# Reordering the middle of a fused attention-and-MLP training step: exponential, wo transposes, d(o) by head, and dV groups between the sums

## The chip, the cores and the metric

The kernel runs on one core of a Trainium2 chip. A core has TensorE (PE), VectorE (DVE), ScalarE (ACT), GpSimd (POOL) and SyncE (SP), each with its own instruction queue, and 16 DMA engines between its on-chip memory (SBUF, and PSUM for PE's results) and HBM. The metric is the device time of one execution in microseconds, less is better; of several runs, the median. The profile and the trace come from one further, profiled execution.

## The reference

One decode token goes through a block with adaptive layer norm. `_f` is the forward pass; the kernel returns its output and the gradients of nine inputs.

```python
mod = (_silu(c) @ w_mod).reshape(1, 6, 1, -1)            # sa, ca, ga, sb, cb, gb
h = _layernorm(x) * (1 + ca) + sa
q = (h @ wq) as 32 heads of 192
o = softmax(q k^T * 192**-0.5) v                          # k, v: 32 x 8192 x 192
x = x + ga * (o @ wo)                                     # x: 1 x 640
h = _layernorm(x) * (1 + cb) + sb
x = x + gb * (h + _gelu(_layernorm(h) @ w3) @ w4)         # w3: 640 x 1536, the shifted branch is zero for one token
_out, _vjp = jax.vjp(_f, A_x, A_k_cache, A_v_cache, A_wq, A_wo, B_w3, B_w4, c, w_mod)
```

All tensors are bfloat16. K and V are 100.7 MB each, and so are their gradients.

## The kernel before

The work has three parts. The **first part** walks over the 32 heads: K and V come in halves of 1.5 MB, DVE and PE form the scores, ACT the exponentials (`E_all`), and PE sums V times the exponentials (`mp`, from the scaled V tiles `vs`). The **last part** walks back from head 31 in 64 steps of half a head. A step `s` multiplies V by d(o) on DVE (`mul_q`, L1028, two quarters), sums the products on PE with an identity matrix (`tree_q`, L1047, 12 matmuls a quarter into `dot_ps`, a pool of one buffer), makes dP (L344) and dS (L1345) on DVE, dK from dS on DVE (`dk_part`, L1063), and dV as eight groups of outer products on PE (`dv_groups`, L1058) that ACT copies out (L1059). dK and dV are stored from POOL, V is loaded from SP; the buffer for step `s + 4` comes free when the second product of step `s + 1` has been read.

The **middle**, from about 530 to 590 us, has to be done once and in sequence: the last heads' softmax, the output projection (`pair_ao`), the second layer norm (`n2_bf`), `w3` (`u_ps`, L817), GELU, `w4` (`h2_ps`, L900), and back: d(g) by twelve DVE pieces (`dg_part`, L504; pieces not yet done are taken in order, so a call with `NF` does all that are left), `du_bf`, d(n2) (`dn_ps`, L904), the backward layer norm in closed form (`pr`, its means, `s4`, `q4`, `qr`) to `dao_bf` (L942), and d(o) for the first pair of heads (`do_mm(TL)`, L1004, from the transposed `wo` of `do_t`, L886). Work that is not in this sequence is put between: `mp` units for head 30 (`m_units`: two `main`, L402, and two `rest`, L407), transposes of w3 (`w3t`, nine calls, L800 and ACT copies L801, two PSUM buffers), scaled V rows on ACT (`vs_act`, L644), the sums of M2 (`m_add`), the blocks of dW4 (`dw4_dve`, L872, twelve of 128 x 640) with their stores, and the small outputs (`dx1_out`, `d_sb_out`).

The order on PE, DVE, ACT and SP is the order of the program text: a manual schedule holds for `ORDER = {PE, DVE, Activation, SP}`. POOL's queue is ordered by the planner. An instruction waits at the head of its engine's queue and holds all behind it. `psB`, which holds `do_ps`, and `psS`, which holds `c_ps` and the means, have one buffer for their tag; `dv_ps` has two.

Between the middle and the loop over steps, the first step's beginning is written out: `mul_q(0, 0)`, four dV groups and their store, `tree_q` of the first quarter, `mul_q(0, 1)`, the products `cx` and their sums `cs` (L1324, L1326), the matmul `c_ps` (L1328), three dW4 blocks, `cpr` (L1331, a scalar for each head that dS needs), `tree_q` of the second quarter, and `mul_q(1, 0)`. In step 0 the loop does the other four groups, and 1 to 7 by the list `gs = [1, 3, None, None, 5, None, 7, None]`.

Of the kernel before, what the change touches and what calls it, by code (L numbers as in the profile page):

```python
# [20 lines left out]
def kernel(  # L21
# [26 lines left out]
    nc = tc.nc  # L48
# [308 lines left out]
    with tc.tile_pool(name="vs", bufs=3) as vsp, tc.tile_pool(name="ft", bufs=2) as ft, \  # L357
# [38 lines left out]
        def m_units(q, kb, vs, mp):  # L396
            j0 = (q % 2) * JQ
            z = q == 3

            def main(lo, hi):  # L400
                for k in range(lo, hi):
                    T_.matmul(mp[:, 0:MW], lhsT=kb[:, j0 + k, 0:P], rhs=vs[:, k, 0:MW], start=(q == 0 and k == 0), stop=(z and k == JQ - 1), skip_group_check=True)  # L402

            def rest(lo, hi):
                for k in range(lo, hi):
                    p0 = 64 * (k % 2)
                    T_.matmul(mp[p0 : p0 + 64, MO : MO + MW], lhsT=kb[:, j0 + k, P:DH], rhs=vs[:, k, 0:MW], start=False, stop=(z and k >= JQ - 2), skip_group_check=True)  # L407
# [101 lines left out]
        with tc.manual_schedule(engines=ORDER):  # L509
# [209 lines left out]
            T_.matmul(po[:, 4:6], lhsT=c32, rhs=os2[:, 2 * DH : 2 * DH + 2], start=True, stop=True)  # L719
            for k in range(3):  # L720
                T_.matmul(po[:, k : k + 1], lhsT=os2[:, k : 2 * DH : 3], rhs=c32[:, 0:1], start=True, stop=True)
            pe.pop(0)()
# [5 lines left out]
            V_.tensor_tensor(out=xP, in0=xP, in1=xc0, op=ALU.add)  # L728
            V_.reciprocal(out=rinv[:, 2 * TL : 2 * TL + 2], in_=po[:, 4:6])
# [50 lines left out]
            dg_part(1)  # L780
# [4 lines left out]
            vs_act(vs3, 3, 8, 12)  # L785
# [43 lines left out]
            V_.tensor_tensor(out=e1, in0=e1, in1=u, op=ALU.mult)  # L829
            dg_part(1)  # L830
            pe.pop(0)()
            pe.pop(0)()
            w3t()
            pe = m_units(3, ky[1], vs3, mp)
            pe.pop(0)()
            w3t()
            pe.pop(0)()
            w3t()
            V_.tensor_scalar(out=w_, in0=w_, scalar1=1.0, scalar2=None, op0=ALU.add)
            V_.reciprocal(out=s_, in_=w_)  # L840
            V_.tensor_tensor(out=g_, in0=s_, in1=u, op=ALU.mult)
            g_bf = col(NF, "g_bf", BF16)
            V_.tensor_copy(out=g_bf, in_=g_)
            V_.scalar_tensor_tensor(out=t_, in0=s_, scalar=-1.0, in1=e1, op0=ALU.add, op1=ALU.mult)
            V_.scalar_tensor_tensor(out=t_, in0=t_, scalar=-1.0, in1=s_, op0=ALU.add, op1=ALU.mult)
            V_.tensor_scalar(out=n2, in0=hx, scalar1=r2[:, 0:1], scalar2=None, op0=ALU.mult)
            V_.tensor_scalar(out=n1, in0=mo[:, 0, :], scalar1=nm, scalar2=r1[:, 0:1], op0=ALU.add, op1=ALU.mult)
            V_.tensor_tensor(out=rho, in0=r1, in1=r2, op=ALU.mult)
            cn = G[:, 3, :]
            V_.tensor_tensor(out=cn, in0=cb1, in1=n1, op=ALU.mult)  # L850
            V_.tensor_copy(out=G[:, 1, :], in_=n2)
# [7 lines left out]
            V_.scalar_tensor_tensor(out=du_bf, in0=t_, scalar=-1.0, in1=d_g, op0=ALU.mult, op1=ALU.mult)  # L859
            pe.pop(0)()  # L860
            pe.pop(0)()
# [3 lines left out]
            w3t()  # L865
            w3t()
# [38 lines left out]
            do_t(TL, 0)  # L905
            do_t(TL, 8)
# [11 lines left out]
            V_.tensor_scalar(out=NW, in0=NW, scalar1=rho[:, 0:1], scalar2=None, op0=ALU.mult)  # L918
            V_.tensor_scalar(out=A1, in0=cb1, scalar1=rho[:, 0:1], scalar2=None, op0=ALU.mult)
# [4 lines left out]
            V_.scalar_tensor_tensor(out=B1, in0=vv, scalar=nr1, in1=dy_c, op0=ALU.mult, op1=ALU.add)  # L924
            V_.tensor_tensor(out=Bg, in0=B1, in1=ga, op=ALU.mult)
            V_.scalar_tensor_tensor(out=du, in0=t_, scalar=-1.0, in1=d_g, op0=ALU.mult, op1=ALU.mult)
            m_add(H1 - 1, mp, mt)
            V_.tensor_copy(out=bo, in_=h2_ps[:, 0:ND])
            dw4_dve(flat(KX), 0, 0, 3)
            pr = col(4 * ND, "pr").rearrange("p (a b) -> p a b", b=ND)  # L930
            V_.tensor_tensor(out=pr, in0=dn_ps[:, None, :].to_broadcast([P, 4, ND]), in1=G, op=ALU.mult)
            ps = mean_mm(pr.rearrange("p a b -> p (a b)"), 4 * ND)
            d_n2, vg = col(ND, "d_n2"), col(ND, "vg")
            V_.tensor_copy(out=d_n2, in_=dn_ps)
            V_.tensor_tensor(out=vg, in0=Ag, in1=dn_ps, op=ALU.mult)
# [7 lines left out]
            dw4_dve(flat(KX), 0, 3, 6)  # L943
# [33 lines left out]
    def load_er(s):  # L977

        er = bst.tile([P, R8, P], BF16, name="er_b", bufs=2)
        h, t = ht(s)  # L980
        r0 = h * J + t * JH
        nc.scalar.dma_start(out=er[0:P:32, :, :].rearrange("r k p -> r (k p)"), in_=eT_d[r0 : r0 + JH, :].rearrange("(r k) p -> r (k p)", r=4))
        return er
# [14 lines left out]
    def do_mm(t, bs=(0, 1)):  # L998
        wT = woT[t]
        ps = psB.tile([P, 512], FP32, name="do_ps", tag="b")  # L1000
        w = PW
        for i in range(ND):
            rhs = wT[:, i * PW : (i + 1) * PW].rearrange("p (c a) -> p c a", c=3)
            T_.matmul(ps[:, 0:w], lhsT=dao_bf[:, i : i + 1].to_broadcast([P, P]), rhs=rhs, start=(i == 0), stop=(i == ND - 1))  # L1004
        for k in bs:
            h = 2 * t + k
            A_.activation(
                out=do_of(h).rearrange("p (a c) -> p a c", c=3),
                in_=ps[:, 0:w].rearrange("p (c a) -> p a c", c=3)[:, 64 * k : 64 * k + 64, :],
                func=ACT.Copy,  # L1010
                scale=rinv[:, h : h + 1],
            )

    wo_l[TL - 1] = load_wo(TL - 1)
    er_l = {0: load_er(0), 1: load_er(1)}

    do_mm(TL, (1, 0))
    V_.tensor_tensor(out=dao, in0=vg, in1=qr, op=ALU.add)
    dx1_out()
    d_sb_out()  # L1020
    dw4_dve(flat(KX), 0, 6, 9)
    dw4_store(flat(KX), 0, 9)
# [294 lines left out]
    ps = psR.tile([P, JH, TS], FP32, name="dot_ps")  # L1317
    mul_q(0, 0)
    dv_groups(dV0, er, do_of(H1), (0, 2, 4, 6))
    dv_store(0, dV0, 0, JQ)  # L1320
    tree_q(ps, 0, 0)
    mul_q(0, 1)
# [3 lines left out]
    V_.reduce_sum(out=cs, in_=cx, axis=AX.X)  # L1326
    c_ps = psS.tile([P, HQ], FP32, name="c_ps", tag="s")
    T_.matmul(c_ps, lhsT=c32, rhs=cs, start=True, stop=True)  # L1328
    dw4_dve(stg0[:, 2 * D :], 9, 9, 12)
    dw4_store(stg0[:, 2 * D :], 9, 3)  # L1330
    V_.scalar_tensor_tensor(out=cpr, in0=c_ps, scalar=32.0, in1=rinv, op0=ALU.mult, op1=ALU.mult)  # L1331
    tree_q(ps, 0, 1)
    mul_q(1, 0)
# [3 lines left out]
    for s in range(NS):  # L1337
# [68 lines left out]
        if nxt:  # L1406
            dv_store(s, dV, JQ if s == 0 else 0, JH)
        else:
            dv_store(s, dV, JQ, JH, nc.sync)
# [42 lines left out]
```

## Time and profile before

| | |
|---|---|
| median of 3 runs (lowest, highest) | 1410.95 us (1407.8, 1412.75) |
| profiled execution, its own time | 1408.49 us |
| its span, first to last instruction | 1406.7 us |
| busy: PE, DVE, ACT, POOL | 85%, 79%, 64%, 8% of the span |
| moved by DMA | 569.36 MB, mean 405 GB/s |
| mean granted clock of TensorE | 0.717 |

The span is what the trace covers; the time adds 1.8 us around it. In the rows of windows, after the length of the stretch, come the busy time of each engine with its number of instructions, the granted clock, the busy share of the 16 DMA engines and GB/s. In the chain of waits a row has its start, its length and the engine, tile and line; `issue` is time in which nothing shown held the engine. A row of the page cut in 40 slices covers 35.2 us with one digit, in tenths.

### The profile page before, as it was taken

To read this page: it belongs to the slowest core of one execution; us is meant where nothing else is said; L and a number is where in the kernel's file an instruction comes from. 1 tells how busy PE (TensorE), PEld (TensorE's weight loads), DVE (VectorE), ACT (ScalarE), POOL (GpSimd) and SP (SyncE) were. 2 spreads that over 40 slices of the span, in tenths; PEclk is the share of its full clock that TensorE was granted. 3 is DMA by queue.
4 is the path that set the end of the run, shared out by engine and by line. 5 is a ranking of instruction groups with operands and counts; after the bars stand their busy time and mean duration, and the time that the engine had idled before them with its cause. 6 is when DMAs were issued, how large, how long until landed. Compare 5 with 4: busy or idle time off the path is not lost.

```text
span 1406.7 us, 30418 instructions
## 1 busy us (share of the span) xinstructions
PE 1191.4 (85%) x12687; PEld 747.4 (53%) x12687; DVE 1111.1 (79%) x1464; ACT 899.3 (64%) x1966; POOL 105.6 (8%) x190
## 2 busy tenths in 40 slices
PE   3898989999998999798766988898989799779875
PEld 2777777777777778543323444443444344334431
DVE  4999999999999997986764875776766777768775
ACT  0777777777777778466644665565656566556664
POOL 0000000000000000110110111101110111101110
PEclk9999999999999999755555555555555555555555
DMA  9999999999999997599999999999999999999998
GB/s 374 394 419 420 417 416 419 410 422 417 421 414 412 408 413 294 192 391 427 424 403 406 426 424 427 421 426 424 426 418 424 421 412 426 412 408 393 425 409 356
DMA packets 76184, 569.36 MB, mean 405 GB/s; under 512 B 7278, under 2 KB 25022, under 8 KB 35982
## 3 DMA queue, kind: packets, MB, share of 16 engines
q1 hardware_dynamic: 51146, 342.02, 59.7%
q0 software_dynamic: 24368, 224.87, 38.3%
q8 instruction: 99, 1.62, 0.4%
q10 hardware_dynamic: 532, 0.53, 0.1%
q14 instruction: 39, 0.32, 0.1%
HBM read 340.95 MB, written 226.43 MB: 403 GB/s over the span
## 4 chain that ended last, share of the span: by engine, by line
issue 44%; DVE 20%; DMA 16%; PE 12%; POOL 5%; ACT 2%; SPq 0%; POOLq 0%; DVEq 0%
DMA KB<-in_A_k_cache_dram 10%; DVE prod L330 8%; DVE prod L334 4%; DMA out_dram<-KB 4%; PE mp L402 3%; DVE vs L380 2%; PE half_ps L340 2%; POOL out_dram L1313 2%; POOL out_dram L1309 2%; DMA w_st<-in_A_wq_dram 2%; PE mp L407 2%; PE dot_ps L1047 1%; DVE pq L1028 1%; PE dv_ps L1058 1%; DVE KB L1063 1%
## 5 line engine op out<-in xcount | busy, mean ns | idle before, releaser
L1059 ACT CAST KB<-dv_ps 128x768 bf16<-128x768 f32 x512 | 397.5, 803 | 165.3 <-PE dv_ps L1058 164.1
L1047 PE MATMUL dot_ps<-pq,ident_bf 128*128 128x256 bf16 x1506 | 386.5, 401 | 26.6 <-DVE dP L344 24.3
L1063 DVE TENSOR_TENSOR KB<-qs_bc,dS 128x3072 bf16<-128x3072 bf16 x122 | 210.6, 1752 | 118.2 <-DMA out_dram<-KB 103.5
L387 ACT ACTIVATE vs<-VB,Ef 128x192 bf16<-128x192 bf16 x840 | 303.5, 447 | 0.0
L1047 PEld LDWEIGHTS <-ident_bf 128*128 128x128 bf16 x1506 | 153.2, 125 | 184.9 <-issue 145.1
L1058 PE MATMUL dv_ps<-do_r,er_b 1*128 1x192 bf16 x2048 | 233.4, 341 | 4.9 <-ACT KB L1059 3.4
L1028 DVE TENSOR_TENSOR pq<-VB,do_r 128x3072 bf16<-128x3072 bf16 x126 | 220.4, 1749 | 16.2 <-PE dot_ps L1047 16.2
L330 DVE TENSOR_TENSOR prod<-KB,qs_bc 128x6144 bf16<-128x6144 bf16 x62 | 207.8, 3352 | 27.0 <-DMA KB<-in_A_k_cache_dram 19.5
L402 PE MATMUL mp<-vs,KB 128*128 128x193 bf16 x1984 | 189.3, 247 | 4.7 <-ACT vs L387 3.1
L402 PEld LDWEIGHTS <-KB 128*128 128x128 bf16 x1984 | 169.0, 97 | 13.7 <-DMA KB<-in_A_k_cache_dram 5.9
L887 ACT COPY wT<-wT_ps 128x1024 bf16<-128x1024 bf16 x82 | 79.0, 963 | 123.2 <-PE wT_ps L886 122.8
L1058 PEld LDWEIGHTS <-er_b 1*128 1x128 bf16 x2048 | 69.8, 105 | 158.5 <-issue 155.5
L340 PE MATMUL half_ps<-prod,ident_bf 128*128 128x256 bf16 x744 | 95.0, 279 | 44.6 <-DVE prod L334 44.1
L380 DVE TENSOR_TENSOR vs<-VB,E 128x1728 bf16<-128x1728 bf16 x120 | 123.6, 1051 | 0.3 <-ACT vs L387 0.3
L334 DVE TENSOR_TENSOR prod<-prod 128x3072 bf16<-128x3072 bf16 x62 | 108.7, 1754 | 1.0
L407 PE MATMUL mp<-vs,KB 128*64 128x193 bf16 x1984 | 106.6, 250 | 0.0
L340 PEld LDWEIGHTS <-ident_bf 128*128 128x128 bf16 x744 | 73.1, 99 | 62.9 <-issue 53.7
L344 DVE TENSOR_REDUCE dP<-dot_ps 128x32 f32<-128x512 f32 x64 | 43.9, 686 | 69.9 <-PE dot_ps L1047 69.8
L367 ACT ACTIVATE E<-S_h,negm 128x256 bf16<-128x256 f32 x31 | 15.8, 508 | 116.1 <-DVE negm L532 113.8
L407 PEld LDWEIGHTS <-KB 128*64 128x64 bf16 x1984 | 79.5, 109 | 19.6 <-issue 19.4
L1313 POOL DMA_DIRECT2D out_dram<-KB x61 | 33.7, 552 | 466.1 <-DVE KB L1063 291.6
L416 PE MATMUL op<-vs,ones_bf 128*32 128x193 bf16 x1920 | 62.1, 250 | 0.0
(356 smaller groups left out, 969.7 us busy)
## 6 DMA issues: line engine op xcount, KB each, us to landing
VB<-in_A_v_cache_dram SPq DMA_DIRECT2D x123, 1536.0 KB
out_dram<-KB POOLq DMA_DIRECT2D x123, 1536.0 KB, 15.8
KB<-in_A_k_cache_dram SPq DMA_DIRECT2D x64, 1536.0 KB
wo_st<-in_A_wo_dram SPq DMA_DIRECT2D x31, 480.0 KB
w_st<-in_A_wq_dram SPq DMA_DIRECT2D x12, 960.0 KB
out_dram<-wo_st POOLq DMA_DIRECT2D x16, 480.0 KB, 16.6
out_dram<-w_st POOLq DMA_DIRECT2D x7, 960.0 KB, 16.0
w_st<-in_w_mod_dram SPq DMA_DIRECT2D x6, 960.0 KB
```

The source lines that it names most:

```text
L330: V_.tensor_tensor(out=prod, in0=src, in1=vec[:, None, :].to_broadcast([P, JH, DH]), op=ALU.mult)
L334: V_.tensor_tensor(out=prod[:, :, 0:HW], in0=prod[:, :, 0:HW], in1=prod[:, :, DH - HW : DH], op=ALU.add)
L340: T_.matmul(ps, lhsT=ident_bf, rhs=prod[:, :, k : k + TF], start=(k == 0), stop=(k == w - TF))
L380: V_.tensor_tensor(out=vs[:, 0:n, 0:DH].rearrange("p j (a b) -> p j a b", b=4), in0=v[:, v0 : v0 + n, :].rearrange("p j (a b) -> p j a b", ...
L387: A_.activation(out=vs[:, k, 0:DH], in_=v[:, v0 + k, :], func=ACT.Copy, scale=Ef[:, j0 + k : j0 + k + 1])
L402: T_.matmul(mp[:, 0:MW], lhsT=kb[:, j0 + k, 0:P], rhs=vs[:, k, 0:MW], start=(q == 0 and k == 0), stop=(z and k == JQ - 1), skip_group_chec ...
L407: T_.matmul(mp[p0 : p0 + 64, MO : MO + MW], lhsT=kb[:, j0 + k, P:DH], rhs=vs[:, k, 0:MW], start=False, stop=(z and k >= JQ - 2), skip_grou ...
L1028: V_.tensor_tensor(out=pq[:, q], in0=v_l[s][:, q * JQ : (q + 1) * JQ, :], in1=do_of(ht(s)[0])[:, None, :].to_broadcast([P, JQ, DH]), op=AL ...
L1047: T_.matmul(ps[:, q * JQ : (q + 1) * JQ, :], lhsT=ident_bf, rhs=pq[:, q, :, k : k + TS], start=(k == 0), stop=(k == w - TS), skip_group_ch ...
L1058: T_.matmul(ps[:, b, k * DH : (k + 1) * DH], lhsT=er[p0 : p0 + 1, 2 * m + k, :], rhs=doh[p0 : p0 + 1, :], start=True, stop=True)
L1059: A_.copy(out=dV4[:, 2 * q : 2 * q + 2, m * PW : (m + 1) * PW], in_=ps[:, :, 0:PW])
L1063: V_.tensor_tensor(out=dK[:, lo:hi, :].rearrange("p j (a b) -> p j a b", b=4), in0=qh.rearrange("p (a b) -> p a b", b=4)[:, None, :, :].to ...
```

## The change

It reorders the middle and the first step. (1) A d_g piece goes ahead of `rinv`, none is left ahead of `n2_bf`, and the pieces around the exponential go behind it. (2) The last eight scaled V rows of the last tile all stand behind `u_ps`: three ahead of the GELU's exponential, five behind it, and the small layer-norm operations go ahead of it. (3) The transposes of wo stand ahead of d(n2) on PE, two dW4 blocks move to ACT, `pr` follows d(n2) at once, and the M2 add goes behind `dao_bf`. (4) `do_mm` can do one head: the last head's d(o) is made alone first, then its neighbour's. The first two loads of `er_b` are issued from SP. (5) All eight dV groups of the first step stand between quarters of its sums, ahead of the loop; `c_ps` and `cpr` follow the groups; nine dW4 blocks and the small outputs move behind the first products.

```diff
@@ output projection
+            m_rest(0, ky[0], vs0, mp, JQ // 2, 13)     # the second `rest` unit in two parts around po
             for k in range(3):
                 T_.matmul(po[:, k : k + 1], lhsT=os2[:, k : 2 * DH : 3], rhs=c32[:, 0:1], start=True, stop=True)
-            pe.pop(0)()
+            m_rest(0, ky[0], vs0, mp, 13, JQ)
...
             V_.tensor_tensor(out=xP, in0=xP, in1=xc0, op=ALU.add)
+            dg_part(1)
             V_.reciprocal(out=rinv[:, 2 * TL : 2 * TL + 2], in_=po[:, 4:6])
...
-            dg_part(1)
             n2_bf = col(ND, "n2_bf", BF16)
...
-            vs_act(vs3, 3, 8, 12)
@@ behind u_ps
-            dg_part(2)
+            dg_part(1)
+            ... n2, n1
             w3t()
-            vs_act(vs3, 3, 12, JQ)
-            w3t()
+            vs_act(vs3, 3, 8, 11)
             ... u, k2, w_, exponential
-            dg_part(1)
+            ... rho, cn, G, sg
+            w3t()
+            vs_act(vs3, 3, 11, JQ)
             ... m_units and w3t in turn
             dg_part(NF)
             du_bf = col(NF, "du_bf", BF16)
@@ d(n2) to dao_bf
             ... h2_ps
+            do_t(TL, 0)
+            do_t(TL, 8)
+            dw4_act(flat(KX), 0, 0, 2)
             ... dn_ps
-            do_t(TL, 0)
-            do_t(TL, 8)
...
+            V_.tensor_copy(out=bo, in_=h2_ps[:, 0:ND])
+            V_.tensor_tensor(out=pr, in0=dn_ps[:, None, :].to_broadcast([P, 4, ND]), in1=G, op=ALU.mult)
+            ps = mean_mm(pr.rearrange("p a b -> p (a b)"), 4 * ND)
             ... A1, nr1, NWg, Ag, B1, vg, Bg
-            m_add(H1 - 1, mp, mt)
-            dw4_dve(flat(KX), 0, 0, 3)
...
             V_.tensor_tensor(out=dao_bf, in0=vg, in1=qr, op=ALU.add)
-            dw4_dve(flat(KX), 0, 3, 6)
+            V_.tensor_copy(out=d_n2, in_=dn_ps)
+            m_add(H1 - 1, mp, mt)
+            dw4_dve(flat(KX), 0, 2, 3)
@@ d(o) and the first step
-    er_l = {0: load_er(0), 1: load_er(1)}
-    do_mm(TL, (1, 0))
-    V_.tensor_tensor(out=dao, in0=vg, in1=qr, op=ALU.add)
-    dx1_out()
-    d_sb_out()
-    dw4_dve(flat(KX), 0, 6, 9)
-    dw4_store(flat(KX), 0, 9)
+    er_l = {0: load_er(0, nc.sync), 1: load_er(1, nc.sync)}
+    do_mm(TL, 1)
+    do_mm(TL, 0)
...
     mul_q(0, 0)
-    dv_groups(dV0, er, do_of(H1), (0, 2, 4, 6))
-    dv_store(0, dV0, 0, JQ)
-    tree_q(ps, 0, 0)
-    mul_q(0, 1)
+    dv_groups(dV0, er, doh, (0, 2))
+    mul_q(0, 1)
+    V_.tensor_tensor(out=dao, in0=vg, in1=qr, op=ALU.add)
+    dw4_dve(flat(KX), 0, 3, 9)
+    dv_groups(dV0, er, doh, (4,))
+    tree_q(ps, 0, 0, 0, 4)
+    dv_groups(dV0, er, doh, (6,))
+    dv_store(0, dV0, 0, JQ)
+    dw4_store(flat(KX), 0, 9)
+    tree_q(ps, 0, 0, 4, 8)
+    dv_groups(dV0, er, doh, (1,))
+    tree_q(ps, 0, 0, 8, 12)
+    dv_groups(dV0, er, doh, (3,))
     ... cx, cs
+    tree_q(ps, 0, 1, 0, 4)
+    dv_groups(dV0, er, doh, (5,))
+    tree_q(ps, 0, 1, 4, 8)
+    dv_groups(dV0, er, doh, (7,))
+    dv_store(0, dV0, JQ, JH)
     T_.matmul(c_ps, lhsT=c32, rhs=cs, start=True, stop=True)
+    tree_q(ps, 0, 1, 8, 12)
+    V_.scalar_tensor_tensor(out=du, in0=t_, scalar=-1.0, in1=d_g, op0=ALU.mult, op1=ALU.mult)
+    V_.scalar_tensor_tensor(out=cpr, in0=c_ps, scalar=32.0, in1=rinv, op0=ALU.mult, op1=ALU.mult)
+    mul_q(1, 0)
     dw4_dve(stg0[:, 2 * D :], 9, 9, 12)
     dw4_store(stg0[:, 2 * D :], 9, 3)
-    V_.scalar_tensor_tensor(out=cpr, in0=c_ps, scalar=32.0, in1=rinv, op0=ALU.mult, op1=ALU.mult)
-    tree_q(ps, 0, 1)
-    mul_q(1, 0)
+    dx1_out()
+    d_sb_out()
@@ loop, step 0
-            gs = [1, 3, None, None, 5, None, 7, None]
+            gs = [None] * 8
```

More of the change, by code (lines that the diff above doesn't have):

```diff
@@ L409, in m_units, with m_rest @@
             return [lambda: main(0, JQ // 2), lambda: main(JQ // 2, JQ), lambda: rest(0, JQ // 2), lambda: rest(JQ // 2, JQ)]
+        def m_rest(q, kb, vs, mp, lo, hi):
+            j0 = (q % 2) * JQ
+            for k in range(lo, hi):
+                p0 = 64 * (k % 2)
+                T_.matmul(mp[p0 : p0 + 64, MO : MO + MW], lhsT=kb[:, j0 + k, P:DH], rhs=vs[:, k, 0:MW], start=False, stop=(q == 3 and k >= JQ - 2), skip_group_check=True)
         def m_quarter(q, kb, vs, mp, op):
@@ L818 @@
             m_add(H1 - 2, z["mp"], mt)
-            dg_part(2)
+            dg_part(1)
+            V_.tensor_scalar(out=n2, in0=hx, scalar1=r2[:, 0:1], scalar2=None, op0=ALU.mult)
+            V_.tensor_scalar(out=n1, in0=mo[:, 0, :], scalar1=nm, scalar2=r1[:, 0:1], op0=ALU.add, op1=ALU.mult)
             w3t()
-            vs_act(vs3, 3, 12, JQ)
-            w3t()
+            vs_act(vs3, 3, 8, 11)
             u, k2, w_, s_, g_, du, e1, t_ = (col(NF, n) for n in ("u", "k2", "w_", "s_", "g_", "du", "e1", "t_"))
@@ L828 @@
             V_.tensor_scalar(out=e1, in0=k2, scalar1=6.0 * GELU_K0, scalar2=2.0 * GELU_K0, op0=ALU.mult, op1=ALU.add)
-            V_.tensor_tensor(out=e1, in0=e1, in1=u, op=ALU.mult)
-            dg_part(1)
[L831 to L847, printed above, removed]
             V_.tensor_tensor(out=rho, in0=r1, in1=r2, op=ALU.mult)
@@ L850 @@
             V_.tensor_tensor(out=cn, in0=cb1, in1=n1, op=ALU.mult)
+            V_.tensor_tensor(out=e1, in0=e1, in1=u, op=ALU.mult)
             V_.tensor_copy(out=G[:, 1, :], in_=n2)
@@ L855 @@
             V_.tensor_tensor(out=sg[:, 3:5, :], in0=nQ, in1=G[:, 3:4, :].to_broadcast([P, 2, ND]), op=ALU.mult)
-            ps5 = mean_mm(sg.rearrange("p a b -> p (a b)"), 5 * ND)
+            w3t()
+            vs_act(vs3, 3, 11, JQ)
+            pe.pop(0)()
+            pe.pop(0)()
+            w3t()
+            w3t()
+            pe = m_units(3, ky[1], vs3, mp)
+            pe.pop(0)()
+            ps5 = mean_mm(sg.rearrange("p a b -> p (a b)"), 5 * ND)
+            w3t()
+            pe.pop(0)()
+            V_.tensor_scalar(out=w_, in0=w_, scalar1=1.0, scalar2=None, op0=ALU.add)
+            V_.reciprocal(out=s_, in_=w_)
+            V_.tensor_tensor(out=g_, in0=s_, in1=u, op=ALU.mult)
+            V_.scalar_tensor_tensor(out=t_, in0=s_, scalar=-1.0, in1=e1, op0=ALU.add, op1=ALU.mult)
+            g_bf = col(NF, "g_bf", BF16)
+            V_.tensor_copy(out=g_bf, in_=g_)
+            V_.scalar_tensor_tensor(out=t_, in0=t_, scalar=-1.0, in1=s_, op0=ALU.add, op1=ALU.mult)
             dg_part(NF)
@@ L859 @@
             V_.scalar_tensor_tensor(out=du_bf, in0=t_, scalar=-1.0, in1=d_g, op0=ALU.mult, op1=ALU.mult)
+            w3t()
             pe.pop(0)()
+            w3t()
             pe.pop(0)()
@@ L864 @@
             e_rows_out(TL, er_ps2, flat(KC)[:, 4 * D : 4 * D + P])
-            w3t()
-            w3t()
             mt = mp_out(H1 - 1, mp)
@@ L900, with dw4_act @@
                     T_.matmul(h2_ps[:, k : k + 1], lhsT=w4r(a)[:, k * P : (k + 1) * P], rhs=g_bf[:, a : a + 1], start=(a == 0), stop=(a == NF - 1))
+            do_t(TL, 0)
+            do_t(TL, 8)
+            def dw4_act(dst, a0, lo, hi):
+                for a in range(lo, hi):
+                    A_.activation(out=dst[:, (a - a0) * D : (a - a0 + 1) * D], in_=dbo_bc, func=ACT.Copy, scale=g_[:, a : a + 1])
+            dw4_act(flat(KX), 0, 0, 2)
             dn_ps = psO.tile([P, 256], FP32, name="dn_ps", tag="op")[:, 0:ND]
@@ L918 @@
             V_.tensor_scalar(out=NW, in0=NW, scalar1=rho[:, 0:1], scalar2=None, op0=ALU.mult)
+            V_.tensor_copy(out=bo, in_=h2_ps[:, 0:ND])
+            pr = col(4 * ND, "pr").rearrange("p (a b) -> p a b", b=ND)
+            V_.tensor_tensor(out=pr, in0=dn_ps[:, None, :].to_broadcast([P, 4, ND]), in1=G, op=ALU.mult)
+            ps = mean_mm(pr.rearrange("p a b -> p (a b)"), 4 * ND)
             V_.tensor_scalar(out=A1, in0=cb1, scalar1=rho[:, 0:1], scalar2=None, op0=ALU.mult)
@@ L924 @@
             V_.scalar_tensor_tensor(out=B1, in0=vv, scalar=nr1, in1=dy_c, op0=ALU.mult, op1=ALU.add)
+            d_n2, vg = col(ND, "d_n2"), col(ND, "vg")
+            V_.tensor_tensor(out=vg, in0=Ag, in1=dn_ps, op=ALU.mult)
             V_.tensor_tensor(out=Bg, in0=B1, in1=ga, op=ALU.mult)
-            V_.scalar_tensor_tensor(out=du, in0=t_, scalar=-1.0, in1=d_g, op0=ALU.mult, op1=ALU.mult)
-            m_add(H1 - 1, mp, mt)
-            V_.tensor_copy(out=bo, in_=h2_ps[:, 0:ND])
-            dw4_dve(flat(KX), 0, 0, 3)
[L930 to L935, printed above, removed]
             V_.tensor_tensor(out=vg, in0=vg, in1=Bg, op=ALU.add)
@@ L975, with load_er @@
     NS = 2 * HQ
-    def load_er(s):
+    def load_er(s, eng=nc.scalar):
         er = bst.tile([P, R8, P], BF16, name="er_b", bufs=2)
@@ L981, in load_er @@
         r0 = h * J + t * JH
-        nc.scalar.dma_start(out=er[0:P:32, :, :].rearrange("r k p -> r (k p)"), in_=eT_d[r0 : r0 + JH, :].rearrange("(r k) p -> r (k p)", r=4))
+        eng.dma_start(out=er[0:P:32, :, :].rearrange("r k p -> r (k p)"), in_=eT_d[r0 : r0 + JH, :].rearrange("(r k) p -> r (k p)", r=4))
         return er
@@ L996, with do_mm @@
     tp_pool.update(p=psT, t="t")
-    def do_mm(t, bs=(0, 1)):
+    def do_mm(t, b=None):
         wT = woT[t]
         ps = psB.tile([P, 512], FP32, name="do_ps", tag="b")
-        w = PW
+        bs = (0, 1) if b is None else (b,)
+        w = DH * len(bs)
         for i in range(ND):
-            rhs = wT[:, i * PW : (i + 1) * PW].rearrange("p (c a) -> p c a", c=3)
+            rhs = wT[:, i * PW : (i + 1) * PW].rearrange("p (c a) -> p c a", c=3)[:, :, 64 * bs[0] : 64 * bs[-1] + 64]
             T_.matmul(ps[:, 0:w], lhsT=dao_bf[:, i : i + 1].to_broadcast([P, P]), rhs=rhs, start=(i == 0), stop=(i == ND - 1))
-        for k in bs:
-            h = 2 * t + k
+        for k, b in enumerate(bs):
+            h = 2 * t + b
             A_.activation(
@@ L1317 @@
     ps = psR.tile([P, JH, TS], FP32, name="dot_ps")
+    doh = do_of(H1)
     mul_q(0, 0)
-    dv_groups(dV0, er, do_of(H1), (0, 2, 4, 6))
-    dv_store(0, dV0, 0, JQ)
-    tree_q(ps, 0, 0)
-    mul_q(0, 1)
+    dv_groups(dV0, er, doh, (0, 2))
[5 more added lines that the diff above has]
+    dv_groups(dV0, er, doh, (6,))
+    dv_store(0, dV0, 0, JQ)
+    dw4_store(flat(KX), 0, 9)
[3 more added lines that the diff above has]
+    dv_groups(dV0, er, doh, (3,))
     cx = bst.tile([P, HQ, ND], FP32, name="v_bc")
@@ L1405 @@
             er_l[s + 2] = load_er(s + 2)
-        if nxt:
-            dv_store(s, dV, JQ if s == 0 else 0, JH)
+        if s == 0:
+            pass
+        elif nxt:
+            dv_store(s, dV, 0, JH)
         else:
```

## The prediction

> **What bounds the kernel now.** I read the slices of the page first, then the middle in a table of windows, then the chain of waits from 568 us on, and the timeline and the waits beside it for single rows.
>
> ```profile
> PEclk9999999999999999755555555555555555555555
> DMA  9999999999999997599999999999999999999998
> ```
>
> The transfers are busy in every slice but those from 527 to 598 us. What a change can win or lose is therefore how long they lack work there.
>
> ```profile
> core 0: us, PE busy (x) PEld busy (x) DVE busy (x) ACT busy (x) POOL busy (x), PEclk, DMA share, GB/s
> 553.00:580.00 27.00, 20.30 (x362) 16.68 (x357) 23.88 (x106) 17.12 (x34) 2.08 (x3) 0.81 0.17 51
> 580.00:594.00 14.00, 10.42 (x114) 7.17 (x112) 13.89 (x19) 5.04 (x8) 2.45 (x4) 0.87 0.92 320
> 594.00:614.00 20.00, 19.13 (x167) 10.75 (x167) 13.49 (x15) 13.49 (x20) 1.07 (x2) 0.67 1.01 416
> 614.00:615.00 1.00, 0.68 (x9) 0.15 (x7) 1.00 (x1) 1.00 (x3) 0.67 (x2) 0.55 0.47 191
> 616.00:624.00 8.00, 7.90 (x46) 3.02 (x46) 7.95 (x9) 4.20 (x7) 1.08 (x2) 0.50 1.01 377
> ```
>
> The transfers idle 0.83 x 27 = 22.4 us to 580, 1.1 us to 594 and another 0.5 us at 614: at 614 they have no stock of work. So the chain of computation sets the time up to there, and a shift of it passes to the end. DVE is full from 580 to 594 (13.89 of 14 us). The chain shows who carries it:
>
> ```profile
> 569.52 1.74 PE dn_ps L904 x60
> 571.27 1.62 PE wT_ps L886 x15
> ...
> 574.22 0.17 DVE dao_bf L942
> 574.39 0.89 DVE KB L872 x3
> ...
> 582.12 0.89 DVE stg L872 x3
> 583.00 0.10 DVE cpr L1331
> 583.10 1.67 DVE pq L1028
> 584.77 0.64 DVE dP L344
> ```
>
> After d(n2) (dn_ps) the transposes of wo stand on the path; from dao_bf on it is DVE without a gap. In this chain the steps are spaced 1.67 us for a product (L1028), 0.89 for three dW4 blocks, 0.72 for dP, 0.27 for dS. The point to follow is the product L1028 of the second half of step 1, now at 585.70: behind it stand dK (3.42), a product and dP, all DVE, then PE's step. No transfer appears in the chain before 634 us.
>
> ```profile
> 616.10 1.01 PE dot_ps L1047 x4
> 617.11 0.43 PE dv_ps L1058 x4
> 617.54 0.97 PE dot_ps L1047 x4
> ```
>
> These later steps are what the change makes of the first one: sums (tree, L1047) and dV groups (L1058) in turn. Four sums with one group cost 0.97 + 0.43 us, at clock 0.50 in the row 616 to 624 although PE is busy 7.90 of 8 us.
>
> **Before dao_bf.** (1) One d_g piece (L504, one per 0.866 us) goes into DVE's wait of 1.26 us for po (547.42, done 548.3, rinv still at 548.68) and one less stands ahead of n2_bf: n2_bf 555.85 to 555.40, u_ps done 557.78 to 557.33. (2) The exponential (561.06) has ahead of it on ACT one copy (0.95) and three scaled-V rows (0.37 each) in place of a copy, four rows and a short copy: it starts at about 560.0. But nine d_g pieces now follow it where there were seven, so du_bf comes at 561.05 + 9 x 0.866 = 568.9 against 569.30. (3) PE and ACT meanwhile pass the w3 transposes through two banks, and ACT has the same rows and copies to do, 557.95 + 9.3 us; the last transposes end at 566.9 (now 566.55), h2 takes 1.55, wo's transposes 1.0 at full clock (15 x 0.065): d(n2) starts at 569.5, where it starts now. Their 1.62 us behind it go off the path. (4) d(n2) ends at 571.2. pr, now at 572.69 behind three dW4 blocks and the M2 add, follows at once, 571.25; but eight small operations stand between it and s4, 0.95 us, longer than the mean (0.37 to 0.62). dao_bf: 572.9. Now: 574.22. Gain 1.3 us.
>
> dW4 blocks 0 and 1 on ACT are not in the trace: between 0.37 (192 columns) and 1.0 (1024), I take 0.67 by width; they fit in ACT's gap of 3 us behind wo's copies, 571.2 to 574.2. Uncovered they cost 1.3.
>
> **d(o).** One head alone has half the columns: five matmuls of 1.76 us become 0.95 (bounds 0.55, at the pace of dV's 192 columns, and 1.76), so 573.15 to 574.1, and its ACT copy ends at 574.5. The pool of do_ps has one buffer: the other head's matmuls wait for that copy and end at 575.5, and the first dV group behind them starts there (now 576.74).
>
> The row loads er_b move from ACT, where their issues took 0.59 and 0.49 us, to SP behind the wo load. eT_d's writes leave POOL 1.5 us later (ACT's copies stand behind nine w3 copies), landing at 572.0 by the 3.0 to 3.4 us shown; er_b issued at 573.07 was in use at 576.74, so it takes at most 3.7. From 572.2 that is 0 to 0.4 us of wait at 575.5; I take 0. Nothing is held up on SP: the next V load waits for L1028 until 587.48.
>
> **The first step.** DVE: d_n2, the M2 add and one dW4 block fit before 574.5. Two products 574.55 to 577.9; dao, six dW4 blocks (1.78), cx and cs (0.75): 580.5. Here comes du and then cpr, which needs c_ps from PE, and DVE runs in order: two products, three blocks, dx1, d_sb and dP queue behind cpr. On PE c_ps stands behind almost the whole woven step. From the end of the first dV copy (575.5 + 0.53 + 0.75, about 576.85) PE has six groups x 0.43, five quarter-trees x 0.97 and c_ps 0.48: 2.6 + 4.85 + 0.5 = 7.95, so 584.8. ACT's copies (0.75 each 1.4 us) don't bind. DVE waits 4.2 us. Now c_ps stood ahead of the second tree and three dW4 blocks hid it (DVE showed no wait for it).
>
> Then: cpr 584.85, product to 586.6, three blocks 587.5, dx1 and d_sb (1.86, 575.19 to 577.05 now) 589.35, dP 0.72, dS 0.27: the product of the second half at 590.3. Now: 585.70. **Sum: +4.6 us.** Even without any wait DVE would come there at 586.15 (+0.45): the 1.3 us won are spent on waiting for d(o) and on the M2 add, du and one more dW4 block behind dao_bf.
>
> The transfers agree. First store: four groups done at 579.5, issued 579.8 behind POOL's usual 0.3 us; the bytes start at 580.6 (now 580.0, with dW4 issued at 578.38). What is ready before V, 3.54 MB at 0.41 MB/us, lasts to 589.3; V is released at 592.1 (now 587.48): about 2.8 us idle more by then, and the rest at 614, where there is no stock. POOL's order of stores changes, but dV (768 KB) first and dW4 (1440 KB) 0.4 us behind it keep the queue filled. The dV groups taken out of step 0's loop free PE and ACT there, where DVE is the bound: nothing.
>
> The profiled execution took 1408.49 us (span 1406.7, 1.8 around it), 2.5 under the median of 1410.95, inside its runs. 1408.49 + 4.6 = 1413.1; on the median, 1410.95 + 4.6 = 1415.5.
>
> **Rivals.** A difference of 0.3% (4.2 us) is about what a measurement can tell here.
>
> (a) The weave runs at full clock. The row 607.69 gives 0.27 for a group and 0.54 for four sums at clock 1.00; then ACT's copies bind and c_ps is there at 581.4, DVE waits 0.9, and the sum is 1.3: 1412.2. The clock came on at 583.4 now, after 24 sums in a row; against it, the row 616 to 624, the same alternation, at 0.50 throughout. [...] 0.14.
>
> (b) Not slower: the clock holds one step later. After step 0, now without dV, PE runs 24 sums in a row (5.4 us), as it did at 579.8 to 584.4 before the clock came on. If it is then on in step 1, whose PE part (593.1 to 603.5 now, at 0.50) falls to DVE's 7.7 us, 2.7 us return; with (a)'s 1.3 that is 1409.5. It decides if the clock is on in both places; on in the second alone: 1412.8. For it: PE has no gap between these sums and step 1. Against: it went off at 593.6 now. 0.11.
>
> (c) More lost: the clock's full stretch from 607.3 to 614.1 does not recur, since the steps fall elsewhere. PE's 2.2 us of sums and groups behind do_ps (607.12 to 609.3) take twice that, and er_b comes 0.4 late: 1418. 0.26.
>
> (d) Something else, such as POOL sending dW4 first, or the early pieces: 0.03, near 1405.
>
> **Numbers.** The main case has 0.46, with its own range from 1413.5 to 1417.5, so 0.30 of it is past 4.2 us (which would be 1415.2) and 0.16 within. Slower: 0.30 + 0.26 = 0.56. Within: 0.16 + 0.14 + 0.06 of (b) = 0.36. Faster: 0.05 of (b), if the clock holds through step 2 too, and (d): 0.08. The range runs from 1410.0, most of (a), to 1420.0, (c) with the uncovered ACT blocks (1.3).
>
> **What would show it.** Right: DVE's longest wait is cpr for c_ps, about 4 us; PEclk 0.50 through the weave; dn_ps at 569.5 with the wo transposes ahead of it; dao_bf near 572.9; V released near 592; more transfer idle between 588 and 594 and at 614 to 620. Wrong: a wait for c_ps under 1 us, a clock of 1.00 between 577 and 585, or transfers starting clearly before 579. Then the gain ahead of dao_bf would stand alone, and the time would be at or below the old one.

## The result and the profile after

The changed kernel takes 1415.97 us (median of 14 runs, 1411.23 to 1419.73) against 1411.41 us (14 runs, 1407.80 to 1414.94) for the kernel before. The ratio is 1.0031, 95% interval 1.0017 to 1.0044: about 4.4 us slower (2.4 to 6.2). The forecast was 1415.5 us. The profiled execution took 1411.23 us, the lowest of the 14 and so not a typical one, with a span of 1409.4 us; the one of before had 1406.7.

The slices of the changed kernel's page show the same picture, transfers busy but for one gap, which is a little deeper (4 for 5 in the slice from 564 to 599 us). The clock falls from 7 to 6 in that slice and rises from 5 to 6 in the next:

```profile
PEclk7899999999999999665555565555555556555555
DMA  9999999999999997499999999999999999999998
```

The table of windows of the changed kernel, for the stretches that were read before:

```profile
core 0: us, PE busy (x) PEld busy (x) DVE busy (x) ACT busy (x) POOL busy (x), PEclk, DMA share, GB/s
553.00:580.00 27.00, 21.90 (x372) 17.46 (x369) 22.19 (x89) 18.98 (x36) 1.07 (x2) 0.82 0.16 51
580.00:594.00 14.00, 9.55 (x49) 5.48 (x50) 9.19 (x25) 3.19 (x4) 2.90 (x4) 0.50 0.75 269
594.00:614.00 20.00, 17.61 (x220) 10.49 (x220) 18.52 (x19) 15.03 (x23) 2.03 (x4) 0.93 0.99 386
614.00:615.00 1.00, 0.67 (x9) 0.23 (x5) 1.00 (x2) 0.94 (x3) 0.68 (x2) 0.50 1.01 430
577.00:585.00 8.00, 8.00 (x49) 3.58 (x46) 3.40 (x13) 5.01 (x7) 1.58 (x2) 0.50 0.42 149
```

From 580 to 594 DVE was full (13.89 of 14 us) and is now busy for 9.19; the transfers' share fell from 0.92 to 0.75, so they idle 3.5 us there instead of 1.1. In 594 to 614 the clock is 0.93 where it was 0.67, and at 614 the transfers no longer idle. The last row is the weave (dV groups and sums in turn): PE busy for all of its 8 us, at clock 0.50.

The chain of waits of the changed kernel (start, length, engine, output, line; rows are left out at the dots, and the short `issue` rows throughout):

```profile
569.17 1.67 PE dn_ps L918 x60
570.86 0.18 DVE pr L933
...
572.48 0.18 DVE dao_bf L950
572.71 0.47 PE do_ps L1015 x2
573.17 1.99 DMA er_b<-eT_d
575.30 0.52 PE dv_ps L1065 x4
...
583.75 0.43 PE dv_ps L1065 x4
584.19 0.58 PE c_ps L1350 x2
584.79 0.19 DVE cpr L1353
584.98 1.67 DVE pq L1035
586.65 0.89 DVE stg L878 x3
...
589.39 0.63 DVE dP L344
...
590.39 1.67 DVE pq L1035
```

The wo transposes are gone from behind `dn_ps`. Between 575.3 and 584.8 the chain is on PE (groups and sums, then `c_ps`) but for one copy on ACT, where before it ran on DVE without a break. DVE's timeline has the wait, in brackets:

```profile
580.06 0.16 DVE L1352 SCALAR_TENSOR_TENSOR du<-t__10313,d_g 128x12 f32<-128x12 f32 x1
584.79 0.19 DVE L1353 SCALAR_TENSOR_TENSOR cpr<-c_ps,rinv 128x32 f32<-128x32 f32 x1 [4.57 <-PE c_ps L1350]
```

In the kernel before, the same instruction ran without a wait:

```profile
582.92 0.18 DVE L1331 SCALAR_TENSOR_TENSOR cpr<-c_ps,rinv 128x32 f32<-128x32 f32 x1
```

In the changed kernel DVE has nothing but `cpr` to go on with and stands for 4.57 us; the product of the second half of step 1 starts at 590.31 (585.70 before), and the next V load is issued at 592.09 (587.48). The transfers have run dry by then and start again behind that load:

```profile
591.00:592.00 1.00, 1.00 (x7) 0.69 (x6) 1.00 (x2) 0.00 (x0) 0.00 (x0) 0.50 0.16 62
592.00:593.00 1.00, 1.00 (x7) 0.69 (x5) 1.00 (x2) 0.00 (x0) 0.00 (x0) 0.50 0.00 0
593.00:594.00 1.00, 1.00 (x6) 0.76 (x5) 1.00 (x2) 0.00 (x0) 0.00 (x0) 0.50 1.07 221
```

The wait also holds back the store of the last three dW4 blocks (588.10 for 583.58); no run frees the one without the other.

### The profile page after: what moved, and what is told of

The parts are those of the page before. It is cut to its first block, busy times and chain, and to the rows that moved or that the text cites. A ratio compares the mean times of both kernels' runs of the same rounds, so it can differ in the third digit from the quotient of the medians.

```text
span 1409.4 us, 30435 instructions
## 1 busy us (share of the span) xinstructions
PE 1183.8 (84%) x12692; PEld 744.0 (53%) x12692; DVE 1111.0 (79%) x1462; ACT 899.6 (64%) x1968; POOL 105.1 (7%) x190
## 4 chain that ended last, share of the span: by engine, by line
issue 38%; DVE 24%; DMA 19%; PE 11%; POOL 5%; ACT 1%; SPq 0%; POOLq 0%; DVEq 0%
DVE prod L330 10%; DMA KB<-in_A_k_cache_dram 9%; DVE prod L334 5%; DMA out_dram<-KB 4%; DVE vs L380 3%; DMA w_st<-in_A_wq_dram 3%; PE mp L402 3%; PE half_ps L340 2%; POOL out_dram L1320 2%; POOL out_dram L1316 2%; DMA stg<-in_A_wq_dram 2%; PE dot_ps L1054 2%; PE mp L407 1%; DMA out_dram<-stg 1%; DVE KB L1070 1%
```

## The experiments

Two explanations were set against each other. **Theory A**, the prediction's: the loss is DVE's wait at `cpr`, through which the second half of step 1 and V's release come late. **Theory B**: the loss is the later restart of the transfers, since the first stores stand behind the woven work. Each kernel was timed against the kernel before; its trace is read from a point that all of them have, the start of the last head's exponential (`E_all`, L710, 544.89 here), because the stretch ahead of it varies by some microseconds from execution to execution (it starts at 543.22 in weave_alone and at 548.07 in short_weave). From there to `dao_bf` the traces still differ: 29.76 and 29.37 us with the old front (before and weave_alone), 26.55 to 28.97 with the changed one. The repeats were timed against their own runs of the kernel before, whose medians were 1411.03, 1410.64 and 1409.45, so the ratios are to be compared and not the medians.

**`cpr` behind the small outputs (cpr_last).** This is the changed kernel with one line moved:

```diff
-    V_.scalar_tensor_tensor(out=cpr, in0=c_ps, scalar=32.0, in1=rinv, op0=ALU.mult, op1=ALU.mult)
     mul_q(1, 0)
     dw4_dve(stg0[:, 2 * D :], 9, 9, 12)
     dw4_store(stg0[:, 2 * D :], 9, 3)
     dx1_out()
     d_sb_out()
+    V_.scalar_tensor_tensor(out=cpr, in0=c_ps, scalar=32.0, in1=rinv, op0=ALU.mult, op1=ALU.mult)
```

> The changed kernel with one line moved: cpr stands behind d_sb_out on DVE, so the second-step product, three dW4 blocks, dx1 and d_sb no longer queue behind its wait for c_ps. Theory A (the loss is DVE's wait for c_ps, 4.6 us): the product waits only for the first quarter's sums (about 581.0), dP for the last sums (585.6), the product L1035 of the second half starts at 586.6 instead of 590.3, V is released near 588.3, and the time is 0.9 us over the kernel before, 1412.3. Theory B (the loss is the later restart of the transfers, 581.6 instead of 580.0, and the wait only stands in the shadow of it): the restart stays, so the time stays 3 us or more over the kernel before, 1414.5 to 1416.

Measured: 1410.86 us (12 runs), ratio 1.000 [0.9984, 1.0015] to the kernel before (1411.03). The loss is gone; theory A's 0.9 us over lies inside the interval (−2.3 to 2.1), theory B's 3 us or more does not. DVE's timeline of this kernel:

```profile
580.09 1.76 DVE L1035 TENSOR_TENSOR pq<-VB,do_r 128x3072 bf16<-128x3072 bf16 x1 [0.96 <-PE dot_ps L1054]
584.50 0.18 DVE L1358 SCALAR_TENSOR_TENSOR cpr<-c_ps,rinv 128x32 f32<-128x32 f32 x1
```

`cpr` runs at 584.50, about where it ran in the changed kernel, but nothing waits behind it: the product runs at 580.09 instead of 584.90. The second half's product comes 40.92 us behind the exponential (45.42 in the changed kernel, 41.24 before), and the transfers idle 0.4 us from 580 to 594, while the first store stays where the change had put it: 7.58 us behind `dao_bf` in both (4.16 before), and nothing ahead of `dao_bf` was changed.

**The front without the weave (front_alone).** The changed kernel with the old first step: groups 0, 2, 4, 6 first, whole trees, `c_ps` ahead of the second tree, `du` just ahead of `cpr`:

```diff
-    dv_groups(dV0, er, doh, (0, 2))
+    dv_groups(dV0, er, do_of(H1), (0, 2, 4, 6))
+    dv_store(0, dV0, 0, JQ)
+    tree_q(ps, 0, 0)
     mul_q(0, 1)
...
-            gs = [None] * 8
+            gs = [1, 3, None, None, 5, None, 7, None]
```

> The changed kernel with the first step in its old order: dx1, d_sb and six dW4 blocks ahead of the first product, four dV groups, c_ps ahead of the second quarter's sums, the other four groups in the loop. Everything ahead of dao_bf and d(o) by head stays as changed. Theory A: the front is a gain of its own, dao_bf at 572.5 (1.7 us earlier), of which the extra work behind it (M2 add, one dW4 block, du) leaves 0.8: the product of the second half at 584.9, time 0.8 us under the kernel before, 1410.6. Theory B: the restart comes with the dW4 store, about 577.6 instead of 578.38, so the same sign; if the time is 3 us or more over the kernel before, the loss is in the front and both theories fall.

Measured: 1410.72 us (12 runs), ratio 0.9999 [0.9984, 1.0014]. `dao_bf` comes 26.57 us behind the exponential (29.76 before) and the second half's product 39.63 (41.24). The product is 1.6 us earlier in this one trace, where 0.8 was expected, but its `dao_bf` is among the earliest of the traces with this front (26.55 to 28.97), so the size of the gain is not sure. The time does not show it; a gain of 0.1% would lie inside the interval.

**The weave without the front (weave_alone).** The kernel before, with the woven first step alone.

```diff
+    doh = do_of(H1)
...
-    dv_groups(dV0, er, do_of(H1), (0, 2, 4, 6))
+    dv_groups(dV0, er, doh, (0, 2))
+    mul_q(0, 1)
+    V_.tensor_tensor(out=dao, in0=vg, in1=qr, op=ALU.add)
+    dw4_dve(flat(KX), 0, 6, 9)
+    dv_groups(dV0, er, doh, (4,))
+    tree_q(ps, 0, 0, 0, 4)
...
-            gs = [1, 3, None, None, 5, None, 7, None]
+            gs = [None] * 8
```

> The kernel before with the woven first step alone (all eight dV groups between the sums, c_ps and cpr behind them); the front and d(o) of both heads together stay as before. Theory A: dao_bf at 574.2, first dV copy done at 578.05, c_ps 7.95 later at 586.0, cpr 586.05, the product of the second half at 591.5: 5.8 us over the kernel before, 1417.2. Theory B: the transfers restart about 1.5 us later than in the changed kernel, 583, and the time is about 3 us over the kernel before, 1414.4.

Measured: 1414.54 us (12 runs), ratio 1.0030 [1.0017, 1.0043], the loss of the whole change. The timeline of DVE has the same wait:

```profile
584.60 0.19 DVE L1340 SCALAR_TENSOR_TENSOR cpr<-c_ps,rinv 128x32 f32<-128x32 f32 x1 [4.43 <-PE c_ps L1338]
```

and its table of windows the same stretch behind it:

```profile
580.00:594.00 14.00, 9.54 (x53) 5.58 (x52) 9.33 (x24) 3.08 (x4) 2.44 (x4) 0.53 0.76 270
```

So the weave carries the loss, and `cpr_last` says which of its lines. The size does not tell the theories apart: the loss is 4.2 us (2.4 to 6.1), and 5.8 (A) and 3 (B) both lie inside. The product came 5.7 us later behind the exponential than before, as A had counted.

**`c_ps` earlier on PE (cps_early).** The changed kernel with the matmul alone moved; DVE's order is untouched, `cpr` included.

```diff
+    c_ps = psS.tile([P, HQ], FP32, name="c_ps", tag="s")
+    T_.matmul(c_ps, lhsT=c32, rhs=cs, start=True, stop=True)
     tree_q(ps, 0, 1, 0, 4)
     dv_groups(dV0, er, doh, (5,))
     tree_q(ps, 0, 1, 4, 8)
     dv_groups(dV0, er, doh, (7,))
     dv_store(0, dV0, JQ, JH)
-    c_ps = psS.tile([P, HQ], FP32, name="c_ps", tag="s")
-    T_.matmul(c_ps, lhsT=c32, rhs=cs, start=True, stop=True)
```

> The changed kernel with c_ps alone moved on PE: ahead of the second quarter's sums (right behind the fourth-last dV group), cpr stays ahead of the second-step product on DVE. Theory A (what counts is when V's buffer is released, and that waits for c_ps): c_ps about 2.8 us earlier, DVE's wait 1.9 instead of 4.6 us, the product of the second half and V's release 2.8 us earlier than in the changed kernel, time 1.8 us over the kernel before or less, 1411 to 1412.8. Theory B (the later first stores): they stay as in the changed kernel, so does the time, 1415 to 1416.

Measured: 1411.24 us (12 runs), ratio 1.0012 [0.9998, 1.0027] to 1410.64. The wait shrinks and does not end, as DVE's timeline has it:

```profile
582.10 0.19 DVE L1353 SCALAR_TENSOR_TENSOR cpr<-c_ps,rinv 128x32 f32<-128x32 f32 x1 [1.73 <-PE c_ps L1345]
```

With 2.8 us less of the wait, 1.7 us of loss (−0.3 to 3.8) is left of 4.4, although the first store stays 7.59 us behind `dao_bf`, as in the changed kernel. The median lies where theory A had it (1411 to 1412.8) and not where B had it (1415 to 1416).

**Two shorter weaves (short_weave, short_weave_2).** Both keep the front, start the stores of dW4 earlier, weave the sums with the dV groups only at the start, put `c_ps` ahead of the second quarter's sums and `dx1_out`, `d_sb_out` into step 1:

```diff
+    dw4_dve(flat(KX), 0, 3, 4)
+    dw4_store(flat(KX), 0, 4)
...
-    tree_q(ps, 0, 1, 0, 4)
-    dv_groups(dV0, er, doh, (5,))
...
     T_.matmul(c_ps, lhsT=c32, rhs=cs, start=True, stop=True)
+    tree_q(ps, 0, 1)
...
+        if s == 1:
+            dx1_out()
+            d_sb_out()
```

The second one also puts the M2 add ahead of `pr`, stores seven blocks of dW4 first, and makes the other head's d(o) (`do_mm(TL, 0)`) only behind the second tree.

> A candidate from both: the changed front; first step with four dV groups between the first quarter's sums and the other four in the loop as before, c_ps ahead of the second quarter's sums, cx and cs right behind the second product, cpr last ahead of dP, dx1 and d_sb behind the product of step 1 in the loop, three dW4 blocks on ACT instead of two, and four dW4 blocks stored at about 573.5, while the transfers idle. Theory A: no wait for c_ps, dP set by the last sums at 583.1, the product of the second half at 584.0, 1.7 us earlier than in the kernel before: 1409.2. Theory B: 640 KB go out in idle time (1.6 us) and the first dV store goes at 579.7: 1.5 to 3 us under the kernel before, 1408 to 1409.5.

Measured: 1410.32 us (12 runs), ratio 0.9998 [0.9986, 1.0009]. The gain that both theories expected (1.5 us and more) cannot be told from none.

> short_weave with three more moves: the M2 add goes into DVE's 0.6 us of idle time ahead of pr (so that er_b's load, which was issued 0.7 us behind dao_bf when that add had read its tile, is free earlier), the neighbour head's d(o) goes behind the sums, and seven dW4 blocks instead of four are made and stored before the first product. From the exponential of head 31 to dao_bf 27.6 us as in the changed kernel; the first dV group at 1.7 us behind dao_bf instead of 2.8; the product of the second half 10.8 to 11 us behind dao_bf (11.8 in short_weave), so 38.5 us behind that exponential against 41.2 in the kernel before. Theory A: V released 2.7 us earlier, time 1.5 to 2.7 us under the kernel before, 1408.5 to 1409.5. Theory B: 1120 KB in idle time and the first dV store 1 us earlier: 2 to 4 us under, 1407 to 1409. If the time is that of the kernel before, something behind the first step takes the gain back.

Measured: 1409.30 us (12 runs), ratio 0.9993 [0.9982, 1.0004] to 1410.64. The first store goes out 29.86 us behind the exponential, 4.1 us earlier than before, and the second half's product comes at 38.44, 2.8 us earlier. The windows of short_weave_2 show that DVE is full again and that the transfers now idle 2.5 us between 580 and 594:

```profile
580.00:594.00 14.00, 10.48 (x118) 6.96 (x116) 13.64 (x22) 6.03 (x9) 3.02 (x5) 0.87 0.82 293
```

Work that was stored sooner here ran out sooner: of 3.9 us less idle ahead of 580, 1.4 come back behind it.

> short_weave_2 once more, unchanged, for a narrower interval against the kernel before (first: 0.9993, 0.9982 to 1.0004). Its idle time of the transfers is 2.6 us less in the first trace, which would be a ratio of 0.998; theory A and theory B both expect 0.998 to 0.999. If it comes at 1.000 or above, the gain of the middle does not reach the end.

Measured: 1409.12 us (12 runs), ratio 1.000 [0.9982, 1.0018] to 1409.45. It beats the changed kernel; against the kernel before no gain can be told, and by the mark that its expectation set, the gain of the middle does not reach the end.

**The changed kernel twice more, for its profile (after_look_1, after_look_2).** Nothing is edited; the question is how steady the clock is behind the weave.

> The changed kernel once more, for a second trace: its first profiled run had the lowest time of 14 (1411.23), with the clock at 1.00 from 595 to 612. Theory A: the wait of cpr for c_ps (4.6 us) and the product of the second half 45 us behind the exponential of head 31 come again in every run; if this run's time is nearer to 1416, the clock is at 0.50 in part of step 1 or 2 and the transfers idle again between 600 and 620. Theory B: the same times in step 1, and the difference between runs lies ahead of 545 us.

Measured: 1412.76 us, span 1411.0. `cpr` waits 4.59 us; the clock is 0.52 from 580 to 594 and 1.00 from 594 to 614, as in the first profile.

> As after_look_1: a third trace of the changed kernel, to see whether the clock's state in steps 1 to 3 or the time ahead of the middle goes with the run's time.

Measured: 1418.35 us, span 1416.6. `cpr` waits 4.44 us, but the clock is 0.66 from 594 to 614, and dP of step 3 comes 73.96 us behind the exponential (70.03 and 71.42 in the other two, 70.91 before). Most of what this execution is longer by lies elsewhere, though: from dP of step 24 to dP of the last step it takes 505.91 us, the first profile 500.29. Its windows late in the last part:

```profile
1000.00:1200.00 200.00, 167.26 (x1221) 81.06 (x1221) 139.41 (x212) 119.32 (x161) 21.80 (x38) 0.53 1.01 415
1200.00:1380.00 180.00, 145.76 (x1098) 68.99 (x1096) 128.98 (x206) 105.73 (x139) 19.69 (x34) 0.53 0.99 402
```

and the same windows of the first profile of the changed kernel:

```profile
1000.00:1200.00 200.00, 165.74 (x1240) 81.95 (x1239) 138.26 (x212) 121.16 (x163) 21.81 (x38) 0.55 1.01 421
1200.00:1380.00 180.00, 149.14 (x1087) 68.71 (x1086) 134.97 (x211) 103.64 (x137) 20.51 (x35) 0.50 1.00 408
```

At 415 and 402 GB/s for 421 and 408 it moved 1.2 and 1.1 MB less in these 380 us, some 5.5 us of work at 0.41 MB/us, of the 7.2 us by which its span is longer. The code there is the same; why the rate was lower is open.

## Why the prediction came out as it did

**What the runs showed.** Moving one DVE line behind others (cpr_last) takes the loss away, moving one matmul (cps_early) leaves 1.7 us of 4.4, and the woven step alone (weave_alone) brings 4.2. In both repairs the first store stays 7.6 us behind `dao_bf`, 3.4 later than before. Theory A stands; B falls.

**Ahead of `dao_bf`.** The exponential started at 560.06 (said 560.0), `du_bf` came at 568.94 (568.9), d(n2) at 569.17 (569.5) with wo's transposes done ahead of it in 1.00 us, `pr` at 570.86 (571.25), `dao_bf` at 572.48 (572.9). The gain, 1.74 us by this trace's clock and 1.3 said, is 2.2 us counted from the exponential; the other traces with this front have 0.8 to 3.2. All of them are earlier than the two traces with the old front, so the sign is well supported; the size is not known to better than a microsecond. The dW4 blocks on ACT took 0.78 us each (0.67 said), in the gap foreseen.

**d(o) and `er_b`.** The first head's d(o) took 0.98 us (0.95), the second ended at 575.16 (575.5), and the first dV group started at 575.30 (575.5). `er_b` was issued at 573.17 and landed 1.99 us later, at 575.16, as the second d(o) ended; it cost 0.1 us at most, so that part of rival (c) did not come.

**The weave.** Said: `c_ps` done at 584.8, DVE waits 4.2, product of the second half at 590.3, V released at 592.1. Measured: 584.77, 4.57, 590.31, 592.09. The bottom-up count of PE's rows at 0.50 was the right term.

Rival (a), the weave at full clock, fails on the window 577 to 585 above (0.50). Behind it, after an idle stretch, stand 24 sums in a row; the timeline of PE:

```profile
590.06 5.28 PE L1054 MATMUL dot_ps<-pq,ident_bf 128*128 128x256 bf16 x24 [4.45 <-DVE dP L344]
```

and the granted clock around their end, in a table of windows of the same kernel:

```profile
594.00:595.00 1.00, 1.00 (x7) 0.61 (x5) 1.00 (x1) 0.00 (x0) 0.00 (x0) 0.50 0.95 393
595.00:596.00 1.00, 1.00 (x30) 0.73 (x32) 1.00 (x2) 0.00 (x0) 0.31 (x1) 0.68 0.98 418
596.00:612.00 16.00, 13.62 (x182) 8.29 (x171) 14.52 (x17) 13.16 (x20) 1.34 (x3) 1.00 0.99 392
```

Behind 5.28 us of sums without groups between them the clock came to 1.00, at about 595.6; in 8 us of sums mixed with one-row outer products, with PE busy throughout, it had stayed at 0.50 (577 to 585). Why it stayed there is not shown; no run took the one-row products out alone.

**The transfers.** V came 4.6 us late as said. POOL sent dW4 ahead of dV, which was rival (d)'s order; the timeline of POOL:

```profile
580.06 1.01 POOL L881 DMA_DIRECT2D out_dram<-KB  x1 [11.06 <-DVE v_bc L1341]
581.07 0.58 POOL L1316 DMA_DIRECT2D out_dram<-KB  x1
```

The transfers so restart 1 us later than forecast, 581.6 for 580.6; by 594 they had idled 2.4 us more than before (2.8 said).

**The last step of the sum is the weak one.** It is "the rest at 614, where there is no stock", that is, that a shift of the product by 4.6 us passes whole to the end. In this profile and in after_look_1 the clock was on in step 1 (0.93 and 1.00 from 594 to 614), as rival (b) had it: here its sums and groups took 0.54 and 0.27 us where 0.97 and 0.43 were counted on. dP of step 3 stands 70.03 us behind the exponential (70.91 before), so the chain had caught up with all 4.2 us, and at 614 the transfers' idle 0.5 us is gone. But the transfer time lost ahead of it (2.4 us by 594) stayed lost. By dP of step 5 the chain is 3 us late again (92.62 for 89.57), behind a wait of DVE for stores out of KB:

```profile
632.50 3.43 DVE L1070 TENSOR_TENSOR KB<-qs_bc,dS 128x3072 bf16<-128x3072 bf16 x2 [5.52 <-DMA out_dram<-KB]
```

At dP of step 24, far from the change, the first profile of the changed kernel is 1.8 us late, near the 2.3 us that its transfers idle more (26.5 for 24.2 from 545 to 640) and the 2.7 by which its span is longer. It was the fastest of 14; after_look_1 and after_look_2 are 3.9 and 4.0 us late there, weave_alone 4.4. So the 4.4 us of the measured ratio are not far from what the other traces show.

The shift at the product does not pass on one for one, and the clock tells the traces apart. Where it was 0.90 or more from 594 to 614 (after, after_look_1, weave_alone, cps_early), the lateness at step 24 is 1.3 to 2.4 us less than the shift of the product; where it was 0.66 to 0.69 (after_look_2, cpr_last, front_alone, the shorter weaves), the two differ by −0.3 to +1.0 us. So what (b) described came in two of three traces of the changed kernel and gave back a part of the 2.7 us that (b) put on it. No run set the clock by itself, there is one trace for each run, and the clock in the other executions is not on record. The forecast of 4.6 was right in place and cause and near in size; the whole shift reached step 24 only in traces whose clock stood at 0.66 to 0.69 from 594 to 614, and that the forecast came out so near the median is in part luck.

Over all kernels the lateness at step 24 (one trace each) goes with the measured ratio on the side of the losses, and hardly on the side of the gains:

| kernel | `cpr` waits, us | second half's product behind the exponential, us | transfers idle 545 to 640, us | dP of step 24 behind the exponential, us | clock, 594 to 614 | ratio to before |
|---|---|---|---|---|---|---|
| before | none | 41.24 | 24.2 | 343.6 | 0.67 | 1 |
| after | 4.57 | 45.42 | 26.5 | 345.4 | 0.93 | 1.0031 [1.0017, 1.0044] |
| after_look_1 | 4.59 | 46.82 | 27.8 | 347.5 | 1.00 | (the same kernel) |
| after_look_2 | 4.44 | 44.25 | 26.8 | 347.6 | 0.66 | (the same kernel) |
| weave_alone | 4.43 | 46.90 | 27.1 | 348.0 | 0.99 | 1.0030 [1.0017, 1.0043] |
| cps_early | 1.73 | 43.93 | 24.7 | 345.0 | 0.90 | 1.0012 [0.9998, 1.0027] |
| cpr_last | none | 40.92 | 23.6 | 343.7 | 0.67 | 1.0000 [0.9984, 1.0015] |
| front_alone | none | 39.63 | 22.3 | 342.3 | 0.69 | 0.9999 [0.9984, 1.0014] |
| short_weave | none | 39.41 | 22.4 | 341.8 | 0.66 | 0.9998 [0.9986, 1.0009] |
| short_weave_2 | none | 38.44 | 21.6 | 340.5 | 0.67 | 0.9993 [0.9982, 1.0004] |
| short_weave_2_again | none | 38.39 | 21.1 | 340.6 | 0.67 | 1.0000 [0.9982, 1.0018] |

Behind step 24 the code is the same in all of them, and yet from there to dP of the last step they take 499.7 to 505.9 us. The trace of the kernel before has 499.8, nearly the least; front_alone and the shorter weaves need 1.5 to 3.3 us more, half or more of what they had won by step 24. Whether that is chance or a cost of coming early is open.

The forecast's count without any wait (+0.45 us at the product) was right in kind: cpr_last comes at −0.3, in a trace whose front is 3.2 us early, and needs 14.34 us from `dao_bf` to the product where the kernel before needs 11.48. So the front's gain is spent in the first step, on work that it takes in ahead of the product and on two waits of DVE there (0.65 us for d(o), 0.96 for the sums). Where the front is kept and the first step is not (front_alone), that way takes 13.06 us, and the 1.6 us left in its trace are too little to measure.

## What to carry to other kernels

When two engines' work is woven together, follow the small operation that reads the last result of the one and stands in the middle of the other's queue: here a 0.19 us instruction made DVE stand for 4.4 to 4.6 us with work ready behind it, and moving that line took the loss away while the weave stayed. Count such a weave at the clock that the same mix shows elsewhere in the trace, not at the clock of a pure run (here 0.50, in 616 to 624 before the change as in the weave, and not the 1.00 that 24 sums in a row came to). Then ask where the shift meets the resource that is full: what is lost there need not equal the shift (here 1.8 us at step 24 for a shift of 4.2 in one trace, whose transfers idled 2.3 us more, and 4.0 for 3.0 in another, where they idled 2.6 more). And take more than one trace: the one at hand may be the fastest of its kernel.

## What had not been expected

The load of `er_b` from SP was not limited by `eT_d`: in the traces of the changed kernel, and of its variants in which the M2 add follows `dao_bf`, its issue comes 0.69 or 0.70 us behind the start of `dao_bf` (573.17 behind 572.48 here), just as the M2 add ends (572.75 + 0.35 = 573.10). That fits a tile whose space the M2 add still reads. short_weave_2, which has that add ahead of `pr`, bears it out: the add ends at 571.32 + 0.35 = 571.67 and the load is issued at 571.76, 1.94 us ahead of `dao_bf`. No run moved the add alone. And the load's 8 KB took 1.99 us from issue to landing in the changed kernel, where the forecast had at most 3.7.
